# Storing rows as whole tiles and loading tokens by stretch in a fused attention, Fourier-mixing and feed-forward kernel

## The chip, the cores and the metric

The kernel runs on one core of one Trainium2 chip. The metric is device time in microseconds (us) of one execution; the time before is the median of three runs. A separate execution was taken with the hardware profiler, and all rows below come from that one.

## The reference

Inputs are q, k, v of 8 batches, 8 heads, 576 positions and 64 dimensions, and two weight matrices, 512x2048 and 2048x512. Per batch and head the attention is the sum of two parts: a pooled one (q, k, v averaged over groups of 4 positions, softmax over all 144 groups, the result repeated 4 times) and a local one (softmax over the 7 positions with |i-j| < 4). Heads are joined to rows x of 512 channels. Then

```
mixed = real(fft(fft(x, axis=1), axis=2))
u  = x + mixed
un = (u - mean(u)) / sqrt(var(u) + 1e-6)        # per row
out = u + max(un @ w_ch1, 0) @ w_ch2
```

## The kernel before

**Attention and mixing, batch by batch.** A batch has five *units* of the local attention (class `Unit`): each covers two windows of 64 positions that lie 57 apart, and gives rows of a tile `x` in SBUF. A window's first three and last three rows only serve as neighbours; the rows that count are 4 to 60 of a window, or 0 to 60 for the first of a half. The second half of a batch is computed in reversed order. Rows of the first half go to the tile `xa`, those of the second half to `xb`, 128 partitions (two windows) by 3 slots by 512 channels. The class `Pooled` computes the pooled part of a batch in four steps of two heads; its result `odt` is moved and stored by L337 to L341. The class `Mix` does the Fourier mixing of a batch: it adds `xa` and `xb` mirrored (`cross`, `fold`), multiplies by a sequence matrix (`sequence`) and a channel matrix (`mix`), and leaves the mixed rows in two tiles `oa` and `ob`.

**Three stores per batch.** What the feed-forward part needs goes to DRAM: `ud` (pooled rows, 1 transfer), `ul` (local rows, L640 to L650, 10 transfers) and `um` (mixed rows, L630 to L637, 5 transfers), in the order of tokens. One of the five for `um`, L635, takes partitions 1 to 127 of `ob`, 127 rows.

**Feed-forward.** The 4608 rows are cut into 36 tiles of 128 and 9 blocks of 4 tiles (class `Block`). A tile is loaded by SP from `ul` (L715), and GpSimd's (POOL's) queue adds `um` (L713) and `ud` (L711) to it by accumulating DMAs, in the order of the four tiles: four times `um`, then four times `ud`. DVE then takes the statistics (`stats`), normalises (`norm`), PE transposes (`turn`), and ACT and DVE split the result in two parts. Per block, 16 steps f follow: `first` (12 matmuls, L770), `high` on ACT, `low` on DVE, `second` (12 matmuls, L788 to L790). While block n is multiplied, block n+1 is loaded and prepared: the load of a tile waits until the output of block n-1 that lies in the same buffer has been stored (L798). The weights come as 64 quarters, four for each f (`raw`, fetched on SP at L150), and are decoded on ACT, POOL and DVE; 8 quarters are decoded during attention, 56 from its end on.

**What sets the order.** Every step is planned at a time in units of its own (the dictionary `AT`, 20 units per batch); all steps are sorted by that time and issued in that order. Each engine's queue, SP's and POOL's among them, runs its instructions in that order and stops at the first one that has to wait. All DMAs but the accumulating and the constant ones are issued by SP. The loads of the next batch's q and k (`qkT`, L367) and v (`vaug`, L371) therefore stand in the same queue as the stores of `um` (planned as `M.store`) and `ul` (`M.store_local`).

Of the kernel before, what the change touches and what calls it, by code (L numbers as in the profile page):

```python
# [8 lines left out]
F32 = mybir.dt.float32  # L9
# [4 lines left out]
ALU = mybir.AluOpType  # L14
# [5 lines left out]

PACE = 20
AT = {

    "pooled": (-1.19, 0.05, -1.8, -2.83, -3.64),
    "mix": (18.82, 18.19, 18.08),

    "local_steps": (0, 1.59, 2.96, 4.87, 6.03, 7.81, 9.34),
    "pooled_steps": (0, 1.56, 3.05, 4.81, 5.73, 7.85, 9.41),

    "qk": (-12.1, 2.19),  # L30
    "sums": (-2.01, 0.44),
    "sum_v": (-13.12, -6.44, -2.59, 2.41),
    "load_v": (0.51,),

    "store_pooled": (0.1, 0.2),
    "crosses": ((1, 4.9), (2, 8.0), (0, 9.2)),
    "folds": ((3, 4.3), (1, 5.9), (2, 8.5), (0, 10.0)),
    "splits": (0.37, 0.9, 1.3),
    "z": (10.2, 12.12, 12.81, 15.82),
    "sequence": (12.92, 1.78, 0.82, 1.82),  # L40
    "mixed": (20.36, 2.6, 0.6, 0.9, 1.5, 2.0, 2.6),
    "store_local": (9.6,),

    "ffn": (4.81, 1.67),

    "decode": (50.65, 9.96, 8.82, 1.2, 1.74),
    "decode_steps": (-1.38, 0.24, 0.83, 1.88, 2.96),
    "first_norms": (1.6, 0.81, 2.43, 1.1),
    "second_norms": (-0.15, 1.47, 0.8, 1.75),

    "add": (13.24, 1.0, 2.2),
}


# [5 lines left out]

TINY_HIGH = 1.125 * 2.0**-15
HUGE_HIGH = 2.0**16 * (1.875 - 2.0**-23)


@with_exitstack
def kernel(
# [34 lines left out]
    HS = S // 2  # L101
# [3 lines left out]

    dram = ctx.enter_context(tc.tile_pool(name="dram", bufs=1, space=DRAM))
    ud = [dram.tile([G, DM], F32, name=f"ud{b}") for b in range(B)]
    ul = [dram.tile([S, DM], F32, name=f"ul{b}") for b in range(B)]
    um = [dram.tile([S, DM], F32, name=f"um{b}") for b in range(B)]

    res = ctx.enter_context(tc.tile_pool(name="res", bufs=1))

# [96 lines left out]
    odt = pd.tile([GX, 2, DM + 2], F32, name="odt")  # L209
# [13 lines left out]
    xab = [[px.tile([P, NSL, DM + 2], F32, name=f"x{j}{i}") for j in "ab"] for i in range(2)]
    for ts in xab:
        for t in ts:
            nc.gpsimd.memset(t[:, :, DM:], 0.0)
        nc.gpsimd.memset(ts[1][W:, NSL - 1, :DM], 0.0)
# [16 lines left out]
    sums = {}  # L244

    class Pooled:
# [86 lines left out]

        def move(self):

            x = xab[self.b % 2][0]
            nc.sync.dma_start(out=odt[GH:GX, 0, :DM], in_=odt[W:GH, 1, :DM])  # L337
            nc.sync.dma_start(out=x[W:, NSL - 1, :DM], in_=odt[:W, 1, :DM])

        def store(self):  # L340
            nc.sync.dma_start(out=ud[self.b].rearrange("(t g) c -> g t c", t=2), in_=odt[:GH, :, :DM])  # L341

        def plan(self):
            b = self.b
# [13 lines left out]
    class Unit:  # L358
# [104 lines left out]

        def result(self):
            full = slice(0, P)
            xa, xb = (x[:, :, :DM] for x in xab[self.b % 2])
# [36 lines left out]
    outs = [P, P, NK1 - 2 * P]  # L503
# [9 lines left out]
    class Mix:  # L513
# [7 lines left out]

        def cross(self, t):
            pq = self.pq[t] = psq.tile([P, 2, HD], F32, name="pq", bufs=3)
            xa, xb = xab[self.b % 2]
# [26 lines left out]
            nc.gpsimd.tensor_sub(out=l, in0=self.x[t], in1=h.bitcast(F32))  # L551

        def split_z(self):
            xa, xb = xab[self.b % 2]
# [68 lines left out]


        def mirror(self, t):
            n = outs[t]
            for o, x in (self.o, self.o[::-1]):
                nc.scalar.copy(out=o[:n, t, HD + 1 :], in_=x[:n, t, HD - 1 : 0 : -1])

        def store(self):  # L630
            oa, ob = self.o
            u = um[self.b]
            nc.sync.dma_start(out=u[: 2 * P].rearrange("(t p) c -> p t c", t=2), in_=oa[:, :2])
            nc.sync.dma_start(out=u[2 * P : HS], in_=oa[: HS - 2 * P, 2])
            nc.sync.dma_start(out=u[HS : HS + P - 1], in_=ob[1:, 0])  # L635
            nc.sync.dma_start(out=u[HS + P - 1 : HS + 2 * P - 1], in_=ob[:, 1])
            nc.sync.dma_start(out=u[HS + 2 * P - 1 :], in_=ob[: HS - 2 * P + 1, 2])  # L637


        def store_local(self):  # L640
            for x, r0, first in zip(xab[self.b % 2], (0, HS - 1), (0, 1)):
                for n2 in range(2):
                    base = r0 + n2 * STEP
                    for lo, hi, n in ((4, 60, NSL - n2), (60, 61, NSL - n2 - (not n2 and not first))):
                        dst = ul[self.b][base + lo : base + hi, :]
                        dst = bass.AP(
                            tensor=dst.tensor, offset=dst.offset, ap=[dst.ap[0], [2 * STEP * DM, n], dst.ap[1]]
                        )
                        nc.sync.dma_start(out=dst, in_=x[n2 * W + lo : n2 * W + hi, :n, :DM])
                nc.sync.dma_start(out=ul[self.b][r0 + first : r0 + 4, :], in_=x[first:4, 0, :DM])  # L650
# [42 lines left out]
    class Block:  # L693
# [134 lines left out]
    folds = dict(AT["folds"])  # L828
# [149 lines left out]
STEP, WINDOW, NPAIR, SEQ, HEADS, DIM = 57, 64, 5, 576, 8, 64  # L978
# [71 lines left out]
```

## Time and profile before

| | |
|---|---|
| median of 3 runs | 1276.24 us (1273.78 to 1283.35) |
| profiled execution | 1278.39 us |
| its span in the trace | 1276.5 us |
| mean granted TensorE clock | 0.916 |
| instructions | 20617 |

The span runs from the first to the last instruction of the trace; the execution's time also holds the 1.9 us around it. The granted clock is a share of TensorE's upper level: 1.0 stands for 2.4 GHz, 0.5 for 1.2 GHz. DMA issues are rows of a queue (SPq, or POOL for GpSimd's) and tell how long the issue held that queue; how long the transfer took is seen in the chain of waits, or in what waited for it.

### The profile page before, as it was taken

The numbers are of one execution on the slowest core, as the hardware profiler recorded it, in microseconds if no ns is written. First come the engines' busy times: TensorE is split into PE (matmuls) and PEld (weight loads), VectorE is DVE, ScalarE is ACT, GpSimd is POOL, SyncE is SP. The second block draws the span as 40 slices with busy tenths as digits, with TensorE's granted clock in tenths as the row PEclk, the third lists the DMA queues.
The fourth block names the chain that finished last, engine by engine and source line by source line (L and its number), as shares of the span: only waits on it lengthen the run. The fifth ranks groups of instructions, "written<-read, shape, count | busy, mean of one in ns | idle before, by whom it ended". The sixth has DMA issues, their size and how long they took to land.

```text
span 1276.5 us, 20617 instructions
## 1 busy us (share of the span) xinstructions
PE 1134.8 (89%) x8304; PEld 950.6 (74%) x8304; DVE 529.4 (41%) x1218; ACT 366.7 (29%) x1102; POOL 276.8 (22%) x405
## 2 busy tenths in 40 slices
PE   5797778667587497999999999999999999999998
PEld 4676666657577375788888888888888888888887
DVE  3666547555464585983322122222222222221111
ACT  2656446364455243441101111111111111111010
POOL 2223223142331653663020020030020110200000
PEclk6778778796878698999999999999999999999999
DMA  9655474565734653445050050060140320500000
GB/s 289 177 161 157 148 223 121 156 178 165 197 94 116 171 139 106 129 130 123 10 131 3 1 132 1 1 132 1 65 68 1 91 42 1 127 6 1 34 1 33
DMA packets 57886, 123.02 MB, mean 96 GB/s; under 512 B 7296, under 2 KB 7424, under 8 KB 57536
## 3 DMA queue, kind: packets, MB, share of 16 engines
q1 hardware_dynamic: 44272, 92.17, 22.8%
q0 software_dynamic: 13520, 29.55, 13.1%
q8 instruction: 65, 1.06, 0.3%
q14 instruction: 29, 0.24, 0.1%
HBM read 89.89 MB, written 30.67 MB: 94 GB/s over the span
## 4 chain that ended last, share of the span: by engine, by line
PE 65%; DMA 16%; DVE 10%; ACT 4%; SPq 2%; issue 2%; POOL 1%; DVEq 0%; ACTq 0%; POOLq 0%
PE hps L770 28%; PE acc L788 10%; PE acc L790 9%; PE acc L789 9%; DMA qkT<-in_qk_dram 6%; DMA vsum<-in_vg_dram 2%; DMA ul<-xa 2%; DMA ul<-xb 2%; PE mix L609 2%; DMA raw<-in_wq_dram 2%; PE avd L313 1%; ACT sb L419 1%; DVE sums L385 1%; DMA um<-ob 1%; DVE wt L176 1%
## 5 line engine op out<-in xcount | busy, mean ns | idle before, releaser
L770 PE MATMUL hps<-unT,w1h 128*128 128x512 f32 x1152 | 312.2, 393 | 1.8 <-DVE unT L750 1.8
L778 DVE SCALAR_TENSOR_TENSOR hl<-hps,hh 128x512 fp32r<-128x512 f32 x144 | 99.2, 689 | 471.3 <-ACT hh L774 471.3
L770 PEld LDWEIGHTS hps<-unT,w1h 128*128 128x128 f32 x1152 | 216.5, 189 | 48.3 <-DVE unT L750 2.3
L788 PE MATMUL acc<-w2h,hh 128*128 128x512 f32 x576 | 228.2, 396 | 9.3 <-ACT hh L774 8.8
L774 ACT ACTIVATE hh<-hps 128x512 fp32r<-128x512 f32 x144 | 86.0, 597 | 510.9 <-PE hps L770 510.9
L790 PE MATMUL acc<-w2h,hl 128*128 128x512 f32 x576 | 225.7, 392 | 0.0
L789 PE MATMUL acc<-w2l,hh 128*128 128x512 f32 x576 | 225.6, 392 | 0.0
L770 PE MATMUL hps<-unT,w1l 128*128 128x512 f32 x576 | 155.7, 392 | 0.0
L788 PEld LDWEIGHTS acc<-w2h,hh 128*128 128x128 f32 x576 | 108.7, 189 | 33.2 <-ACT hh L774 9.2
L790 PEld LDWEIGHTS acc<-w2h,hl 128*128 128x128 f32 x576 | 108.5, 188 | 23.9 <-DVE hl L778 0.2
L770 PEld LDWEIGHTS hps<-unT,w1l 128*128 128x128 f32 x576 | 108.7, 189 | 23.6
L789 PEld LDWEIGHTS acc<-w2l,hh 128*128 128x128 f32 x576 | 108.8, 189 | 22.3
L726 POOL TENSOR_TENSOR rstd<-rstd,mhalf 128x1 f32<-128x1 f32 x36 | 20.3, 563 | 294.0 <-DVE rstd L725 294.0
L713 POOL DMA_DIRECT2D ut<-um x40 | 35.8, 1071 | 210.0 <-DMA ut<-ul 209.4
L385 DVE TENSOR_REDUCE sums<-qkT 128x224 f32<-128x896 f32 (+4 forms) x48 | 44.6, 949 | 70.1 <-DMA qkT<-in_qk_dram 69.6
L460 PE MATMUL av<-vaug,pT 64*64 64x65 f32 x1280 | 38.0, 262 | 38.4 <-DMA vaug<-in_vw_dram 36.4
L419 ACT ACTIVATE sb<-sc,mx 128x64 f32<-128x64 f32 x320 | 69.8, 329 | 1.3
L460 PEld LDWEIGHTS av<-vaug,pT 64*64 64x64 f32 x1280 | 31.0, 168 | 46.7 <-issue 41.2
L571 PE MATMUL y<-seqm,fh 128*128 128x290 f32 (+1 forms) x256 | 48.9, 341 | 16.0 <-DVE odt L328 7.3
L571 PEld LDWEIGHTS y<-seqm,fh 128*128 128x128 f32 (+1 forms) x256 | 42.7, 224 | 19.0 <-issue 8.4
L551 POOL TENSOR_TENSOR fl<-xeo,fh 128x512 fp32r<-128x512 f32 (+1 forms) x32 | 43.5, 1361 | 49.0 <-ACT fh L544 49.0
L268 PE MATMUL sp<-sums 64*72 64x144 f32 x256 | 29.8, 348 | 26.7 <-DVE sums L385 17.3
(97 smaller groups left out, 1414.5 us busy)
## 6 DMA issues: line engine op xcount, KB each, us to landing
qkT<-in_qk_dram SPq DMA_DIRECT2D x40, 512.0 KB
raw<-in_wq_dram SPq DMA_DIRECT2D x64, 256.0 KB
vaug<-in_vw_dram SPq DMA_DIRECT2D x40, 260.0 KB
out_dram<-ut SPq DMA_DIRECT2D x36, 256.0 KB
ut<-ul SPq DMA_DIRECT2D x32, 256.0 KB
ut<-um POOLq DMA_DIRECT2D x32, 256.0 KB, 5.7
ut<-ud POOLq DMA_DIRECT2D x32, 256.0 KB, 5.7
vsum<-in_vg_dram POOLq DMA_DIRECT2D x24, 292.5 KB, 7.3
```

Source lines behind the costliest of these rows:

```text
L385: nc.vector.tensor_reduce(out=to, in_=x[:, :, a - g0 : e - g0], axis=AX.X, op=ALU.add)
L419: nc.scalar.activation(out=self.sb[:, hp, h2], in_=sc[:, hp], func=AF.Exp, scale=0.125, bias=self.mx[:, h2, hp : hp + 1],)
L460: nc.tensor.matmul(av[n2 * W : (n2 + 1) * W, hp, :], pT[r, hp, n2], va[r, n2, hp, :], start=True, stop=True)
L551: nc.gpsimd.tensor_sub(out=l, in0=self.x[t], in1=h.bitcast(F32))
L571: nc.tensor.matmul(y, l, r, start=(i == 0), stop=(i == len(mms) - 1))
L713: nc.gpsimd.dma_start(out=u[r0 : r0 + m], in_=um[b][k0 : k0 + m, :], accum_op=ALU.add)
L770: nc.tensor.matmul(hps, a[:, c, :], unT[:, x, c, :], start=(i == 0), stop=(i == len(mms) - 1))
L774: nc.scalar.activation(out=hh, in_=self.hps[f], func=AF.Relu)
L778: nc.vector.scalar_tensor_tensor(out=hl, in0=self.hps[f], scalar=0.0, in1=self.hh[f].bitcast(F32), op0=ALU.max, op1=ALU.subtract)
L788: nc.tensor.matmul(acc, hh, w2h, start=start, stop=False)
L789: nc.tensor.matmul(acc, hh, w2l, start=False, stop=False)
L790: nc.tensor.matmul(acc, hl, w2h, start=False, stop=stop)
```

## The change

**Stores.** `xa` and `xb` become the two halves of one tile `x`, and `oa` and `ob` those of one tile `o`. `ul[b]` is now laid out as slot, half, partition, channel, and gets whole tiles, the rows that don't count included: one transfer of 128 partitions by 4 x 2 KB (1 MB) and one of 64 partitions by 2 x 2 KB (256 KB). `um[b]` is laid out as half, row: for each half one transfer of 128 partitions by 2 x 2 KB (512 KB) and one of 33 rows (66 KB). So 6 transfers instead of 15; `ud` is as before.

**Loads.** A tile's rows are picked out of `ul` by stretch, a stretch being the run of tokens that one window holds (61 or 57). `even_rows` shortens a piece until its number of rows has a divisor from 12 to 16 (or until it has 16 rows at most), and the rest is a piece of its own: 57 rows become 56 and 1. The loads from `um` are cut where a half ends.

**Order.** Most numbers of `AT` are changed. The pooled part of batch 0 moves 2.34 units later, so that on every engine its steps stand behind those of the local units that they stood ahead of; on SP, P0.move and P0.store stand behind one load of v and behind P2.sum_v0. In the other batches neighbouring steps change places. The fetches of quarters 9 and 10 stand ahead of the loads of block 1 on SP. The formulas for the loads and preparation of blocks 2 to 8 are unchanged; the step of the feed-forward plan goes from 1.67 to 1.64 units.

```diff
-    "pooled": (-1.19, 0.05, -1.8, -2.83, -3.64),
-    "mix": (18.82, 18.19, 18.08),
+    "pooled": (1.15, 0.05, -1.8, -2.74, -3.55),
+    "mix": (18.82, 18.55, 17.92),
...
-    "ffn": (4.81, 1.67),
-    "decode": (50.65, 9.96, 8.82, 1.2, 1.74),
+    "ffn": (3.75, 1.64),
+    "decode": (49.49, 9.96, 8.98, 1.2, 1.74),
...
-    "add": (13.24, 1.0, 2.2),
+    "add": (14.25, 2.77, 2.2),
...
+def even_rows(m):
+    while m > 16 and max(k for k in range(1, 17) if m % k == 0) < 12:
+        m -= 1
+    return m
...
-    ul = [dram.tile([S, DM], F32, name=f"ul{b}") for b in range(B)]
-    um = [dram.tile([S, DM], F32, name=f"um{b}") for b in range(B)]
+    ul = [dram.tile([NSL, 2, P, DM], F32, name=f"ul{b}") for b in range(B)]
+    um = [dram.tile([2, NSL * P, DM], F32, name=f"um{b}") for b in range(B)]
...
         def store(self):
-            oa, ob = self.o
-            u = um[self.b]
-            nc.sync.dma_start(out=u[: 2 * P].rearrange("(t p) c -> p t c", t=2), in_=oa[:, :2])
-            nc.sync.dma_start(out=u[2 * P : HS], in_=oa[: HS - 2 * P, 2])
-            nc.sync.dma_start(out=u[HS : HS + P - 1], in_=ob[1:, 0])
-            nc.sync.dma_start(out=u[HS + P - 1 : HS + 2 * P - 1], in_=ob[:, 1])
-            nc.sync.dma_start(out=u[HS + 2 * P - 1 :], in_=ob[: HS - 2 * P + 1, 2])
+            n = HS + 1 - 2 * P
+            for i in range(2):
+                u = um[self.b][i]
+                STORE.dma_start(out=u[: 2 * P].rearrange("(t p) c -> p t c", p=P), in_=self.o[:, i, : NSL - 1])
+                STORE.dma_start(out=u[2 * P : HS + 1], in_=self.o[:n, i, NSL - 1])
...
         def store_local(self):
-            for x, r0, first in zip(xab[self.b % 2], (0, HS - 1), (0, 1)):
...
+            x = xab[self.b % 2][:, :, :, :DM]
+            u = ul[self.b].rearrange("t j p c -> p (t j) c")
+            STORE.dma_start(out=u[:, :4], in_=x[:, :2].rearrange("p t j c -> p (t j) c"))
+            STORE.dma_start(out=u[:W, 4:], in_=x[:W, 2])
...
+                j, k = k0 // HS, k0 % HS
+                m = min(e - g, HS - k)
+                to = P - (e - g)
                 if part == 2:
+                    m = min(e - g, S - k0)
...
                 elif part:
-                    nc.gpsimd.dma_start(out=u[r0 : r0 + m], in_=um[b][k0 : k0 + m, :], accum_op=ALU.add)
+                    nc.gpsimd.dma_start(out=u[to : to + m], in_=um[b][j, k + j : k + j + m, :], accum_op=ALU.add)
                 else:
-                    nc.sync.dma_start(out=u[r0 : r0 + m], in_=ul[b][k0 : k0 + m, :])
+                    n = max(k + j - 4, 0) // STEP
+                    m = even_rows(min(m, STEP * n + STEP + 4 - k - j))
+                    r = k + j - STEP * n + (n % 2) * W
+                    nc.sync.dma_start(out=u[to : to + m], in_=ul[b][n // 2, j, r : r + m, :])
```

## Rows read from the trace of the kernel before

**Rows 1.** The page, its parts 1, 2 and 4: busy time and share of the span of each engine, the clock granted to TensorE in 40 slices of 31.9 us, and the shares of the chain that ended last.

```profile
PE 1134.8 (89%) x8304; PEld 950.6 (74%) x8304; DVE 529.4 (41%) x1218; ACT 366.7 (29%) x1102; POOL 276.8 (22%) x405
...
PEclk6778778796878698999999999999999999999999
...
PE 65%; DMA 16%; DVE 10%; ACT 4%; SPq 2%; issue 2%; POOL 1%; DVEq 0%; ACTq 0%; POOLq 0%
```

**Rows 2.** The chain of waits from 90 to 250 us, in order of time: start, length, what; the pieces of one batch that are no engine's work.

```profile
108.04 14.70 DMA um<-ob
122.75 5.95 DMA ul<-xb
...
129.67 9.19 DMA qkT<-in_qk_dram
```

**Rows 3.** The timeline of SP's own queue in the same batch: start, time the issue held SP, line, destination and source, count.

```profile
107.33 0.33 SPq L634 DMA_DIRECT2D um<-oa  x1
107.72 0.27 SPq L635 DMA_DIRECT2D um<-ob  x1
108.04 4.00 SPq L636 DMA_DIRECT2D um<-ob  x1
112.16 0.52 SPq L637 DMA_DIRECT2D um<-ob  x1
113.12 0.37 SPq L367 DMA_DIRECT2D qkT<-in_qk_dram  x1
113.56 2.73 SPq L649 DMA_DIRECT2D ul<-xa  x4
122.11 0.27 SPq L650 DMA_DIRECT2D ul<-xa  x1
```

**Rows 4.** Who waited for whom from 98.6 to 364.2 us, five batches: total us, times, longest.

```profile
DVE sums L385 <- DMA qkT<-in_qk_dram: 61.6, 18, 8.5
```

**Rows 5.** Busy time of the engines in three stretches, each bounded by two moves of the pooled rows (L337): one batch, five batches, and one of those five. Columns: stretch, its length, busy us (instructions) of PE, PEld, DVE, ACT, POOL, granted clock, DMA share, GB/s.

```profile
53.70:98.60 44.90, 39.24 (x562) 34.10 (x554) 29.08 (x81) 26.41 (x99) 12.35 (x18) 0.78 0.56 159
98.60:364.20 265.60, 194.45 (x2850) 171.69 (x2850) 151.65 (x425) 135.63 (x501) 74.07 (x107) 0.79 0.58 165
204.70:252.10 47.40, 32.92 (x525) 28.77 (x526) 28.70 (x81) 26.43 (x100) 13.59 (x20) 0.88 0.64 180
```

**Rows 6.** The timeline of SP at the end of attention, after the last local rows are computed.

```profile
422.45 2.95 SPq L649 DMA_DIRECT2D ul<-xa  x4
...
430.39 2.37 SPq L649 DMA_DIRECT2D ul<-xb  x4
...
433.76 2.72 SPq L715 DMA_DIRECT2D ut<-ul  x5
```

**Rows 7.** The chain of waits from 405 to 536 us, where decoding and the first FFN blocks run.

```profile
485.03 9.10 DMA raw<-in_wq_dram
...
508.80 2.71 DMA raw<-in_wq_dram
```

**Rows 8.** The timeline of PE: matmuls before which PE stood idle (in brackets: us idle and what ended it), and one group of the same matmuls, L460, without a wait before it.

```profile
14.67 1.24 PE L268 MATMUL sp<-sums 64*72 64x144 f32 x8 [9.38 <-DVE sums L385]
...
235.51 1.16 PE L460 MATMUL av<-vaug,pT 64*64 64x65 f32 x29 [4.70 <-DMA vaug<-in_vw_dram]
...
409.28 0.70 PE L460 MATMUL av<-vaug,pT 64*64 64x65 f32 x32
...
456.60 0.66 PE L741 MATMUL tpn<-ident,un 128*128 128x128 f32 x4 [2.05 <-DVE un L733]
...
495.49 0.80 PE L788 MATMUL acc<-w2h,hh 128*128 128x512 f32 x1 [8.80 <-ACT hh L774]
```

**Rows 9.** Busy time and granted clock (the number after POOL) in a stretch right behind the last of those waits.

```profile
497.00:499.00 2.00, 2.00 (x6) 1.58 (x5) 1.90 (x5) 1.17 (x3) 1.20 (x2) 0.50 0.07 16
```

**Rows 10.** The timelines of SP, POOL, DVE and PE while block 3 is loaded beside block 2's matmuls, and the same pair of rows (norm, turn) in two later blocks.

```profile
652.66 2.75 SPq L715 DMA_DIRECT2D ut<-ul  x5
656.36 1.77 POOL L713 DMA_DIRECT2D ut<-um  x2 [27.20 <-DMA ut<-ul]
661.83 3.55 POOL L711 DMA_DIRECT2D ut<-ud  x4 [0.36 <-issue]
667.64 0.69 DVE L722 BATCH_NORM_STATS2 st<-ut 128x6 f32<-128x512 f32 x1 [1.15 <-DMA ut<-ud]
669.48 0.55 DVE L733 TENSOR_SCALAR un<-ut,mv,rstd 128x512 f32<-128x512 f32 x1 [0.75 <-POOL rstd L726]
670.41 0.60 PE L741 MATMUL tpn<-ident,un 128*128 128x128 f32 x4
...
759.25 0.55 DVE L733 TENSOR_SCALAR un<-ut,mv,rstd 128x512 f32<-128x512 f32 x1 [0.73 <-POOL rstd L726]
759.87 0.64 PE L741 MATMUL tpn<-ident,un 128*128 128x128 f32 x4
...
936.59 0.55 DVE L733 TENSOR_SCALAR un<-ut,mv,rstd 128x512 f32<-128x512 f32 x1 [0.73 <-POOL rstd L726]
938.77 0.60 PE L741 MATMUL tpn<-ident,un 128*128 128x128 f32 x4
```

**Rows 11.** DMA issues on SP that touch the stored local rows: issue time in ns (shortest, median, longest), first and last start.

```profile
L715 SPq DMA_DIRECT2D ut<-ul x40: 319/408/1017, 287.7 to 1103.3; - x40
L649 SPq DMA_DIRECT2D ul<-xa x32: 398/600/1274, 58.4 to 424.8; - x32
```

More of the change, by code (lines that the diff above doesn't have):

```diff
@@ L22 @@
 AT = {
-    "pooled": (-1.19, 0.05, -1.8, -2.83, -3.64),
-    "mix": (18.82, 18.19, 18.08),
-    "local_steps": (0, 1.59, 2.96, 4.87, 6.03, 7.81, 9.34),
-    "pooled_steps": (0, 1.56, 3.05, 4.81, 5.73, 7.85, 9.41),
+    "pooled": (1.15, 0.05, -1.8, -2.74, -3.55),
+    "mix": (18.82, 18.55, 17.92),
+    "local_steps": (0, 1.66, 2.96, 4.76, 5.65, 7.95, 9.34),
+    "pooled_steps": (0, 1.56, 3.05, 4.81, 5.63, 7.85, 9.33),
     "qk": (-12.1, 2.19),
-    "sums": (-2.01, 0.44),
-    "sum_v": (-13.12, -6.44, -2.59, 2.41),
+    "sums": (-2.36, 0.44),
+    "sum_v": (-12.96, -6.64, -4.76, 2.36),
     "load_v": (0.51,),
     "store_pooled": (0.1, 0.2),
[L36 to L42, printed above, removed]
-    "ffn": (4.81, 1.67),
-    "decode": (50.65, 9.96, 8.82, 1.2, 1.74),
-    "decode_steps": (-1.38, 0.24, 0.83, 1.88, 2.96),
-    "first_norms": (1.6, 0.81, 2.43, 1.1),
-    "second_norms": (-0.15, 1.47, 0.8, 1.75),
-    "add": (13.24, 1.0, 2.2),
+    "crosses": ((1, 4.59), (2, 7.41), (0, 9.2)),
+    "folds": ((3, 5.97), (1, 4.28), (2, 8.26), (0, 10.0)),
+    "splits": (0.74, 0.9, 1.64),
+    "z": (9.51, 12.03, 12.81, 15.82),
+    "sequence": (12.92, 1.78, 0.82, 1.66),
+    "mixed": (20.32, 2.6, 0.2, 0.9, 1.47, 2.03, 2.91),
+    "store_local": (9.66,),
+    "ffn": (3.75, 1.64),
+    "decode": (49.49, 9.96, 8.98, 1.2, 1.74),
+    "decode_steps": (-1.47, 0.24, 0.83, 2.1, 2.96),
+    "first_norms": (0.57, 0.81, 2.43, 0.6),
+    "second_norms": (0.03, 1.47, 0.8, 1.83),
+    "add": (14.25, 2.77, 2.2),
 }
@@ L80 @@
     nc = tc.nc
+    STORE = nc.sync
     P = 128
@@ L220, in bank @@
         return banks[-1].tile([P, DM], F32, name=name, tag="ps")[:rows]
[L223 to L227, printed above, removed]
+    xab = [px.tile([P, NSL, 2, DM + 2], F32, name=f"x{i}") for i in range(2)]
+    for x in xab:
+        nc.gpsimd.memset(x[:, :, :, DM:], 0.0)
+        nc.gpsimd.memset(x[W:, NSL - 1, 1, :DM], 0.0)
     def pooled_at(b):
@@ L334, in move @@
         def move(self):
-            x = xab[self.b % 2][0]
-            nc.sync.dma_start(out=odt[GH:GX, 0, :DM], in_=odt[W:GH, 1, :DM])
-            nc.sync.dma_start(out=x[W:, NSL - 1, :DM], in_=odt[:W, 1, :DM])
+            x = xab[self.b % 2]
+            STORE.dma_start(out=odt[GH:GX, 0, :DM], in_=odt[W:GH, 1, :DM])
+            STORE.dma_start(out=x[W:, NSL - 1, 0, :DM], in_=odt[:W, 1, :DM])
         def store(self):
-            nc.sync.dma_start(out=ud[self.b].rearrange("(t g) c -> g t c", t=2), in_=odt[:GH, :, :DM])
+            STORE.dma_start(out=ud[self.b].rearrange("(t g) c -> g t c", t=2), in_=odt[:GH, :, :DM])
         def plan(self):
@@ L465, in result @@
             full = slice(0, P)
-            xa, xb = (x[:, :, :DM] for x in xab[self.b % 2])
+            xa, xb = (xab[self.b % 2][:, :, i, :DM] for i in range(2))
             if self.m < 2:
@@ L523, in cross @@
             pq = self.pq[t] = psq.tile([P, 2, HD], F32, name="pq", bufs=3)
-            xa, xb = xab[self.b % 2]
+            xa, xb = (xab[self.b % 2][:, :, i] for i in range(2))
             for i, (u, v) in enumerate(((xa, xb), (xb, xa))):
@@ L553, in split_z @@
         def split_z(self):
-            xa, xb = xab[self.b % 2]
+            xa, xb = (xab[self.b % 2][:, :, i] for i in range(2))
             z = self.z = psq.tile([P, NSL + 1, 2], F32R, name="z", bufs=1)
@@ L613, in copy_odd @@
             if self.o is None:
-                self.o = [pf.tile([P, NSL, DM], F32, name=f"o{part}", bufs=2) for part in "ab"]
-            nc.scalar.copy(out=self.o[1][: outs[t], t, : HD + 1], in_=self.ps[t, 1][:, : HD + 1])
+                self.o = pf.tile([P, 2, NSL, DM], F32, name="o", bufs=2)
+            nc.scalar.copy(out=self.o[: outs[t], 1, t, : HD + 1], in_=self.ps[t, 1][:, : HD + 1])
         def join(self, t):
@@ L619, in join @@
             even = self.ps[t, 0][:, : HD + 1]
-            oa, ob = (o[:n, t, : HD + 1] for o in self.o)
+            oa, ob = (self.o[:n, i, t, : HD + 1] for i in range(2))
             for o, op in ((oa, ALU.add), (ob, ALU.subtract)):
@@ L626, in mirror @@
             n = outs[t]
-            for o, x in (self.o, self.o[::-1]):
-                nc.scalar.copy(out=o[:n, t, HD + 1 :], in_=x[:n, t, HD - 1 : 0 : -1])
+            for i in range(2):
+                nc.scalar.copy(out=self.o[:n, i, t, HD + 1 :], in_=self.o[:n, 1 - i, t, HD - 1 : 0 : -1])
         def store(self):
-            oa, ob = self.o
-            u = um[self.b]
-            nc.sync.dma_start(out=u[: 2 * P].rearrange("(t p) c -> p t c", t=2), in_=oa[:, :2])
-            nc.sync.dma_start(out=u[2 * P : HS], in_=oa[: HS - 2 * P, 2])
-            nc.sync.dma_start(out=u[HS : HS + P - 1], in_=ob[1:, 0])
-            nc.sync.dma_start(out=u[HS + P - 1 : HS + 2 * P - 1], in_=ob[:, 1])
-            nc.sync.dma_start(out=u[HS + 2 * P - 1 :], in_=ob[: HS - 2 * P + 1, 2])
-        def store_local(self):
-            for x, r0, first in zip(xab[self.b % 2], (0, HS - 1), (0, 1)):
[L642 to L650, printed above, removed]
+            n = HS + 1 - 2 * P
+            for i in range(2):
+                u = um[self.b][i]
+                STORE.dma_start(out=u[: 2 * P].rearrange("(t p) c -> p t c", p=P), in_=self.o[:, i, : NSL - 1])
+                STORE.dma_start(out=u[2 * P : HS + 1], in_=self.o[:n, i, NSL - 1])
+        def store_local(self):
+            x = xab[self.b % 2][:, :, :, :DM]
+            u = ul[self.b].rearrange("t j p c -> p (t j) c")
+            STORE.dma_start(out=u[:, :4], in_=x[:, :2].rearrange("p t j c -> p (t j) c"))
+            STORE.dma_start(out=u[:W, 4:], in_=x[:W, 2])
         def plan(self):
@@ L706, in load @@
                 b, k0 = g // S, g % S
-                m = min(e - g, S - k0)
-                r0 = P - (e - g)
+                j, k = k0 // HS, k0 % HS
+                m = min(e - g, HS - k)
+                to = P - (e - g)
                 if part == 2:
+                    m = min(e - g, S - k0)
                     groups = ud[b][k0 // 4 : (k0 + m) // 4, :].unsqueeze(1).to_broadcast([m // 4, 4, DM])
-                    nc.gpsimd.dma_start(out=u[r0 : r0 + m], in_=groups, accum_op=ALU.add)
+                    nc.gpsimd.dma_start(out=u[to : to + m], in_=groups, accum_op=ALU.add)
                 elif part:
-                    nc.gpsimd.dma_start(out=u[r0 : r0 + m], in_=um[b][k0 : k0 + m, :], accum_op=ALU.add)
+                    nc.gpsimd.dma_start(out=u[to : to + m], in_=um[b][j, k + j : k + j + m, :], accum_op=ALU.add)
                 else:
-                    nc.sync.dma_start(out=u[r0 : r0 + m], in_=ul[b][k0 : k0 + m, :])
+                    n = max(k + j - 4, 0) // STEP
+                    m = even_rows(min(m, STEP * n + STEP + 4 - k - j))
+                    r = k + j - STEP * n + (n % 2) * W
+                    nc.sync.dma_start(out=u[to : to + m], in_=ul[b][n // 2, j, r : r + m, :])
                 g += m
```

## The prediction, made before the changed kernel was run

> **What bounds the kernel now.** I read the page first. PE is busy 89% of the span, but the granted clock stays at 0.9 or more only from slice 17 on, 510 us [rows 1]: behind lies feed-forward, where PE has hardly a gap, before it attention, mixing and decoding, where it has. A change in storing can win only there, and lose anywhere. The chain of waits gives 16% of the span (204 us) to DMAs [rows 1], so I followed it through one batch: from 108 to 139 us no engine is its bottleneck. A transfer to um (L636's) takes 14.70 us, then one to ul 5.95, then a load of qkT 9.19 [rows 2].
>
> SP's queue says why. L635 (254 KB, 127 partitions) is issued in 0.27 us; the next issue holds SP 4.00 us instead of some 0.33, and the eighth DMA behind L635 (one each of L636, L637 and qkT, four of L649, then L650) starts only at 122.11, when that transfer has landed [rows 2, 3]. At the end of attention, with no qkT load between, the eighth is the first store of xb, and it too waits until 430.39 [rows 6]. So SP has eight DMAs in flight, and the ninth waits for the first. What stands behind is the next batch's qkT, and DVE, in whose queue the sums of qkT stand, waits 61.6 us for it in five batches [rows 4]. L635's 254 KB thus took 14.4 us (107.72 to 122.11), 18 GB/s, and L636, issued behind it, landed no sooner; a whole 256 KB tile of weights takes 2.71 us [rows 7].
>
> The Trainium skill, "DMA: Bandwidth & Descriptors", section "Why a DMA increments its semaphore by 16 and not by 1", gives the reason: a DMA runs on the largest k up to 16 engines that divides its outer size, and 127 rows give k = 1. The trace agrees as far as 18 GB/s goes; by its rate of about 27 GiB/s per engine (an estimate) 9 us would do, and the gain below would be a third smaller.
>
> **Part 1, stores.** 15 transfers become 6, none of 127 rows; the odd ones have 33 rows, like L637, which takes 0.52 us to issue [rows 3]. Bytes hardly change (um 1156 KB as before, ul 1280 for 1136). The L635 wait goes in each batch.
> *Five batches* (98.6 to 364.2). Upper bound: DVE's whole 61.6 us. But something comes next. The batch before them, with ul stores and no um stores, ran in 44.9 us, PE busy 39.2 of it [rows 5]; five such are 225 us against 265.6. That is -41. Lower bound: the one batch of the five that took 47.4 us in spite of the wait shows that waits overlap other work, and its own excess over 44.9 is 2.5; I put the weak end at -20, half.
> *End of attention.* From 417.92 to 433.2 SP is in the last stores; then the loads of block 1 begin [rows 6]. Six transfers at 0.6 us end some 12 us earlier; 1.25 MB then need up to 8 us to land at the mean 165 GB/s [rows 5], so the loads begin 4 to 12 us earlier, 9 say. Block 1 now needs 21 pieces instead of 5 loads (part 2), +7 us, felt by the fetches behind them, but not by those of quarters 9 and 10, now ahead: I count 4. Together -5, between -10 and 0.
> *Last um stores*, among the weight fetches: the raw issued behind L637 takes 9.10 us, and PE stands idle 8.80 us [rows 7, 8]; behind it PE runs at half clock (0.50) for 4 us [rows 9], 2 us more. Taken: -9, between -11 and -4, as four stores still stand there.
>
> **Part 2, loads.** Cutting tokens 0 to 4607 by the new code gives 180 loads on SP instead of 40, 18 to 22 per block for blocks 2 to 8 (mean 20), and 48 um loads on POOL instead of 40. The place where this counts is the start of each block. In block 3's loading, SP begins at 652.66; um starts at 656.36; POOL's queue runs four um issues and then ud, whose first starts at 661.83, 9.2 us after SP; the statistics wait for it on DVE until 667.64, norm ends at 670.03, and PE turns at 670.41 [rows 10]. The slack is 0.4 us; in block 4 it is 0.07, in block 6 1.6 [rows 10]. PE's queue is in order, so nearly every us by which the first ud comes later is a us of PE, seven times (blocks 2 to 8), plus whatever `low` of the running block, behind the statistics on DVE, adds.
> New offset of that ud: 19 spacings on SP + landing of the last piece + um issues of the last tile + a gap of 0.36. Spacing c: issues of ut<-ul have a median of 408 ns, stores in pieces 600 ns [rows 11], and back to back a row every 0.39 us is possible (107.33 to 107.72) [rows 3]; I take 0.45, nearest to the same line's row, between 0.39 and 0.67. Landing: 2.7 us [rows 7], for 3.7 with four whole tiles at once. um issues: 0.88 each (1.77 for 2 [rows 10]), 1.4 on average, 1.3 us. So 8.6 + 2.7 + 1.3 + 0.36 = 12.9. Then 5.8 to the statistics and 2.4 to the end of norm: 21.1 us after SP begins, where PE turns at 17.75. A stall of 3.3 us per block, 23 in seven. Bounds: with c 0.39 and a landing of 2.2 us, 12; with c 0.67, 52.
> *Clock.* A gap of 2.05 us cost PE no clock, one of 4.70 did (29 matmuls of L460 then took 1.16 us, where 32 took 0.70 without a wait) [rows 8]. 3.3 lies between: +7, between 0 and 14 (2 us per block).
> *Block 0* is loaded during attention, 19 pieces for 4: 15 more at 0.45 us in front of qkT loads, in four places where SP mostly waits for engines anyway: +1, between 0 and 5.
>
> **Part 3, order.** Batch 0's pooled steps, all of them and its three DMAs, go behind local units. PE's first idle, 9.38 us waiting for sums [rows 8], can now hold local scores; against that, P0.move stands behind P2.sum_v0 on SP, which waits for the buffer that P0's last values free, so just before P0.move's own data: 1 us at most. The other exchanges are between neighbours. No row prices them; bounded by that idle and by one DMA landing: -2, between -8 and +5.
>
> **Sum** against the profiled execution of 1278.4: -41 - 5 - 9 + 23 + 7 + 1 - 2 = -26, so 1252. It lies 2.2 above the median of the runs, so I predict 1250.
>
> **Rivals.**
> *A, the pieces hide.* Issue at 0.39 and quick landing leave about 1.7 us per block, no clock loss, and attention comes nearer to the 61.6: -52 - 5 - 9 + 12 - 2 + 1 = -55, 1223 (median basis 1221). For: SP is idle before each block, small loads land fast. Against: zero slack in most blocks.
> *B, the wait moves on.* With qkT in time, batches take 49 us instead of 45 because PE and DVE are in order and the um stores still wait for ACT: -21 - 5 - 9 + 31 - 2 = -6, 1272 (1270). For: DVE and ACT are half busy in every batch and hand over to each other [rows 5]. It also covers the case that the 33-row transfers or whole tiles bring no quicker SP.
> *C, slower: the pieces on SP at the head of each block.* If a piece costs 0.67 us, as the stores in pieces did, the stall is 7.5 us plus 2 of clock, 66 in seven, block 1 gets 5 more and block 0 5: -41 - 2 + 0 - 9 + 66 + 5 = +19, 1297 (1295). It decides from about 0.56 us a piece, where the seven stalls eat the 54 us won. For: the local rows' stores, pieces of 56 rows and of one, held SP 600 ns [rows 11]. The Trainium skill, "DMA: Bandwidth & Descriptors", section "Rules for kernel authors", says the same: coalesce many small transfers, as those under 64 KB are mostly overhead. At the 2 us of fixed cost that its section "Anatomy of one DMA" gives for GpSimd's DMAs, one after another, 20 pieces would be 40 us per block and the kernel far slower; but eight are in flight at once [rows 3], which makes it 5 us, below the issue time, and leaves the sum.
>
> **How the numbers follow.** Forecast 0.45, A 0.25, B 0.15, C 0.15. Predicted 1250. The forecast's own range is 1228 to 1270 from the terms' bounds, not all at one end. The range for 8 in 10 takes in most of A and B and leaves out the far half of C: 1217 to 1284. A measurement here can tell about 1% from no change, 12.8 us, so faster means under 1263.5 and slower over 1289: faster 0.25 (A) + 0.35 (forecast) + 0.03 (B) = 0.63; same 0.10 + 0.11 + 0.03 (C) = 0.24; slower 0.12 (C) + 0.01 = 0.13.
>
> **What would show it.** Right, if no issue of SP holds 4 us in the um stores, DVE's wait for qkT falls from 61.6 to under 15 us, and the moves of the pooled rows come about 45 us apart. The stall shows as PE idle before `turn` of the first tile of blocks 2 to 8, released by DVE's norm, near 3 us each, and as first ud issues near 13 us after SP's first piece; A if there is none, C if they are 7 us or more with the clock at 0.50 behind. The forecast fails if batches stay above 50 us, or if the blocks, now 89.5 us apart (759.87 and 938.77 are two of them [rows 10]), come more than 97 apart.

## The result and the profile after

The changed kernel takes 1199.64 us (median of 4 runs, 1195.84 to 1203.31); the kernel before, beside it, takes 1275.12. The ratio is 0.9395 [0.9344, 0.9447]: 75 us faster, where 26 were forecast, and below the range of 1217 to 1284. The profiled execution of after took 1203.31 us, its span is 1201.5. A trace is of one execution, which can lie off its kernel's median (1234.27 for 1226.42 with the old order below, 1289.33 for 1277.60 with the old um), so a few us between two traces say little.

The page of after, the lines of [rows 1]:

```profile
PE 1108.2 (92%) x8304; PEld 927.0 (77%) x8304; DVE 526.5 (44%) x1218; ACT 366.0 (30%) x1102; POOL 277.8 (23%) x411
...
PEclk9788899997978999999999999999999999999999
...
PE 55%; DMA 8%; SPq 4%; DVE 3%; issue 1%; POOL 1%; ACT 0%; POOLq 0%; DVEq 0%; ACTq 0%
```

The same 8304 matmuls keep PE busy for 26.6 us less, and the share of DMAs in the chain of waits is halved. I cut both spans at the same events: the moves of the pooled rows (L337, one per batch) and the first `turn` of blocks 2 and 8.

| stretch | before | after | difference | in the forecast's sum |
|---|---|---|---|---|
| to the first move | 53.7 | 52.3 | -1.4 | (order: -2 in all) |
| one batch | 45.0 | 40.4 | -4.6 | none |
| five batches | 265.6 | 198.6 | -67.0 | -41 |
| last batch | 46.8 | 34.4 | -12.3 | none |
| last move to block 2's first turn, less that turn's stall | 197.1 | 177.9 | -19.2 | -14 |
| stall there, block 2's first turn to block 8's, to the end | 668.4 | 697.9 | +29.5 | +30 (and +1 for block 0, loaded during attention) |

The batches, by the view of [rows 5]: stretch, length, busy us (instructions) of PE, PEld, DVE, ACT, POOL, granted clock, DMA share, GB/s.

```profile
52.30:92.70 40.40, 37.15 (x558) 32.23 (x554) 27.09 (x76) 26.58 (x98) 12.65 (x19) 0.81 0.61 175
92.70:291.30 198.60, 169.99 (x2864) 149.93 (x2858) 150.68 (x425) 134.07 (x499) 70.67 (x108) 0.91 0.75 224
291.30:325.70 34.40, 30.91 (x566) 27.95 (x557) 23.35 (x76) 25.31 (x94) 14.07 (x20) 1.00 0.59 157
```

Against [rows 5], PE's busy time in five batches fell from 194.5 to 170.0 at nearly the same number of matmuls (2850 and 2864 in the trace), as the granted clock rose from 0.79 to 0.91; its idle time fell from 71.1 to 28.6. So 24.5 of the 67.0 us are shorter matmuls, about what the clock gives (194.5 times 0.79 by 0.91 is 169), and 42.5 are gaps that closed.

SP's own queue in the second of these batches, and at the end of attention (start, time the issue held SP, line, what):

```profile
99.58 0.32 SPq L635 DMA_DIRECT2D um<-o  x1
99.94 0.38 SPq L634 DMA_DIRECT2D um<-o  x1
100.43 0.72 SPq L635 DMA_DIRECT2D um<-o  x1
101.19 0.53 SPq L367 DMA_DIRECT2D qkT<-in_qk_dram  x1
101.77 0.80 SPq L641 DMA_DIRECT2D ul<-x  x1
102.61 0.65 SPq L642 DMA_DIRECT2D ul<-x  x1
103.36 1.74 SPq L371 DMA_DIRECT2D vaug<-in_vw_dram  x1
...
334.00 3.83 SPq L151 DMA_DIRECT2D raw<-in_wq_dram  x3
337.93 9.13 SPq L712 DMA_DIRECT2D ut<-ul  x21
```

In [rows 3] the stretch from L635 to the last ul store took from 107.72 to beyond 122; here the stores and the qkT load are through in 3.7 us (99.58 to 103.26). At the end block 1's loads begin 12.2 us behind the last move (337.93 less 325.73), before 22.8 [rows 6]: 10.6 sooner, where I had 9.

The waits of after, for [rows 4] (the five batches, then the trace from 505 to 1042 us; total us, times, longest):

```profile
DVE sums L385 <- DMA qkT<-in_qk_dram: 15.2, 9, 4.9
...
PE tpn L738 <- DVE un L730: 20.8, 7, 4.5
```

The second line is the price of the pieces: a wait that PE did not have in blocks 2 to 8 before.

### The profile page after: what moved, and what is told of

It is laid out like the page before. It is cut to its first block, busy times and chain, and to the rows that moved or that the text cites. A ratio compares the mean times of both kernels' runs of the same rounds, so it can differ in the third digit from the quotient of the medians.

```text
span 1201.5 us, 20868 instructions
## 1 busy us (share of the span) xinstructions
PE 1108.2 (92%) x8304; PEld 927.0 (77%) x8304; DVE 526.5 (44%) x1218; ACT 366.0 (30%) x1102; POOL 277.8 (23%) x411
## 4 chain that ended last, share of the span: by engine, by line
PE 55%; DMA 8%; SPq 4%; DVE 3%; issue 1%; POOL 1%; ACT 0%; POOLq 0%; DVEq 0%; ACTq 0%
PE hps L767 26%; PE acc L785 9%; PE acc L786 9%; PE acc L787 9%; DMA ut<-ud 4%; DMA ut<-ul 3%; SPq L712 3%; DVE ut L791 1%; PE tpn L738 1%; PE mix L609 1%; POOL ut L707 1%; DVE st L719 1%; DVE hl L775 0%; DVE un L730 0%; ACT hh L771 0%
## 5 line engine op out<-in xcount | busy, mean ns | idle before, releaser
L785 PEld LDWEIGHTS acc<-w2h,hh 128*128 128x128 f32 x576 | 109.7, 190 | 22.8
L707 POOL DMA_DIRECT2D ut<-um x48 | 41.9, 1006 | 237.0 <-DMA ut<-ul 200.3
L738 PE MATMUL tpn<-ident,un 128*128 128x128 f32 x144 | 25.6, 309 | 35.1 <-DVE un L730 35.1
L744 ACT CAST unT<-tpn 128x512 fp32r<-128x512 f32 x36 | 21.1, 586 | 118.1 <-PE tpn L738 118.1
L738 PEld LDWEIGHTS tpn<-ident,un 128*128 128x128 f32 x144 | 19.5, 158 | 42.5 <-DVE un L730 38.5
L551 POOL TENSOR_TENSOR fl<-xeo,fh 128x512 fp32r<-128x512 f32 (+1 forms) x32 | 41.6, 1303 | 28.6 <-ACT fh L544 28.6
L571 PE MATMUL y<-seqm,fh 128*128 128x290 f32 (+1 forms) x256 | 44.3, 318 | 4.0 <-DVE x L479 3.1
L313 PE MATMUL avd<-vsum,ptd 72*72 72x65 f32 x512 | 42.2, 239 | 6.3 <-DMA vsum<-in_vg_dram 6.3
```

Of the source, the lines that this page charges most:

```text
L313: nc.tensor.matmul(av[:, t, hl, :], self.pts[h0][hl][:, kt, t * GH : (t + 1) * GH], self.vs[:, kt, h0 + hl, :], start=(kt == 0), stop=(kt ...
L571: nc.tensor.matmul(y, l, r, start=(i == 0), stop=(i == len(mms) - 1))
L707: nc.gpsimd.dma_start(out=u[to : to + m], in_=um[b][j, k + j : k + j + m, :], accum_op=ALU.add)
L738: nc.tensor.transpose(tp[:, c * P : (c + 1) * P], self.un[i][:, c * P : (c + 1) * P], ident)
L785: nc.tensor.matmul(acc, hh, w2h, start=start, stop=False)
```

## The experiments

Each ratio is to the kernel before, run beside it (medians of 1276.84 to 1277.22; 1275.12 beside after). "Five batches" is the stretch between the moves of [rows 5].

| kernel | us | ratio | five batches | DVE waits for qkT in them | last batch |
|---|---|---|---|---|---|
| before | 1276 | 1 | 265.6 | 61.6 | 46.8 |
| before, 127 rows split | 1208.54 | 0.948 | 220.6 | 19.8 | 38.4 |
| before, new um | 1207.98 | 0.9452 | 221.5 | 17.9 | 40.0 |
| before, new order | 1262.04 | 0.9885 | 261.7 | 72.8 | 45.6 |
| after, old order | 1226.42 | 0.9604 | 202.9 | 6.2 | 39.8 |
| after | 1199.64 | 0.9395 | 198.6 | 15.2 | 34.4 |
| after, old um | 1277.60 | 1.0019 | 248.0 | 61.6 | 44.0 |
| before, L635 on ACT's queue | 1287.30 | 1.007 | 267.2 | 69.4 | 49.2 |
| before, ul loads in pieces | 1323.31 | 1.0385 | 267.9 | 66.1 | 46.4 |
| after, preparation later | 1172.97 | 0.9197 | 197.8 | 15.8 | 34.4 |
| after, ud sooner | 1209.65 | 0.9492 | 196.0 | 13.1 | 34.4 |
| after, no `even_rows` | 1290.99 | 1.0103 | 197.7 | 17.3 | 35.0 |
| before, new um and order, later | 1192.01 | 0.933 | 210.1 | 24.0 | 35.8 |

### Which store held attention up

**Only the 127-row transfer cut**, into 112 and 15 rows; all else as before.

```diff
-            nc.sync.dma_start(out=u[HS : HS + P - 1], in_=ob[1:, 0])
+            nc.sync.dma_start(out=u[HS : HS + 112], in_=ob[1:113, 0])
+            nc.sync.dma_start(out=u[HS + 112 : HS + P - 1], in_=ob[113:, 0])
```

> The kernel before, old order, with only the 127-row store cut into 112 and 15 rows (16 transfers per batch instead of 15; the loads stay whole). Theory S (that one transfer is the cause): the attention part gains what the change gained and the feed-forward part pays nothing for pieces: 1178 to 1200 us. Rival N (it is the number of transfers on SP, 15 against 6, that cost): 1255 to 1278 us.

One DMA more, and 68 us less: 0.948 [0.9416, 0.9543], 9 us above the range expected and far from the rival's. The view of the DMA engines tells why. Its first line, shown here, gives the busy share of the 16 engines in 40 slices, in tenths (here 0.4 us each). Before, 107 to 123 us (the stretch of [rows 3]):

```profile
DMA  1015100100000188559897999995897742100001
```

The same view of 16 us around the stores (106 to 122) with the transfer split:

```profile
DMA  2005397895899957989758999975888779799994
```

And of after (99 to 115):

```profile
DMA  9987799997794979999999999999999999999999
```

Before, the engines stand nearly still twice, while SP is held in L636's issue (108 to 112) and again from about 120 on, until L635 has landed at 122.11. One engine of 16 is 0.06 of them, and the share there is 0 to 1 tenth. The Trainium skill, "DMA: Bandwidth & Descriptors", section "Why a DMA increments its semaphore by 16 and not by 1", would put 127 rows on one engine and 112 on sixteen; the rows agree.

**The new um alone** in the kernel before (tile of halves, four stores, loads cut at the half).

> The kernel before, old order, with the new layout, stores and loads of um alone (4 transfers instead of 5, none of 127 rows); ul stays in the order of tokens with its 10 transfers. Theory S: as the split, 1175 to 1200 us, because ul's ten stores cost SP time but no wait. Rival N: 1245 to 1270 us.

0.9452 [0.9407, 0.9497], as with the split alone, and again 8 us above the expected range. So um's part of the change is worth what the 127-row transfer cost; the fewer transfers add nothing here.

**The order alone**, and **the changed kernel with the old order**: only the dictionary `AT` exchanged.

> The kernel before with the new numbers of AT alone; stores and loads as before. Theory S (the stores did it: the 127-row transfer on one DMA engine is gone, order is minor): 1265 to 1285 us, DVE's wait for qkT still near 60 us in five batches, batches still about 53 us. Rival O (the new order is what made batches of 39.7 us, where the stores alone would have given 45): 1240 to 1255 us.

> The changed kernel with the old numbers of AT: new stores, new loads. Theory S: 1193 to 1212 us, five batches still within 10 us of the 198.6 us that the changed kernel takes for them. Rival O: 1220 to 1235 us, batches near 45 us.

Alone the order gives 14.8 us, 0.9885 [0.9844, 0.9927], between the two ranges expected; on the new storage 26.8 (1226.42 to 1199.64), some 12 either way. By its time the changed kernel with the old order falls in rival O's range, by its batches (202.9, or 40.6 each, not 45) in theory S's: the order is not minor, but the short batches come from the stores. By the spans of the two kernels (31.0 us apart) the order is 3.7 to the first move, 2.6 in the next batch, 4.3 in the five, 5.4 in the last, 8.1 between block 2's and block 8's first turns (543.2 to 535.1), and 6.9 in what is left.

With these the five batches add up: the new um -44.1 (265.6 to 221.5), the new ul behind it, old order still, -18.6 (to 202.9), the order -4.3 (to 198.6). The -18.6 goes with a shorter queue on SP: with the split, the ten ul stores still hold SP from 109.59 to 117.99, 8.4 us, where the two of after take 1.5 (above), and DVE's wait for qkT falls from 17.9 to 6.2. That this is its cause is argued; no run changed the ul stores alone.

### Two ways from the slow transfer to qkT

In [rows 2, 3] the slow transfer could delay qkT in two ways: it holds one of eight places, and the ninth DMA waits (my prediction's account), or the transfers behind it wait on the one engine for their own share. Two kernels tell these apart. **The old um in the changed kernel**, with two ul stores behind the 127 rows:

> The changed kernel with the old layout, stores and loads of um, the 127-row transfer among them; ul and order as changed. Only two ul stores stand behind it, so the eighth DMA behind it comes much later in SP's queue. If the wait for one of eight places in flight is what cost, most of the gain stays: 1205 to 1225 us. If the transfer also holds up every other transfer that uses its DMA engine, qkT lands late all the same: 1245 to 1275 us.

**L635 issued from ACT's queue** in the kernel before:

```diff
-            nc.sync.dma_start(out=u[HS : HS + P - 1], in_=ob[1:, 0])
+            nc.scalar.dma_start(out=u[HS : HS + P - 1], in_=ob[1:, 0])
```

> The kernel before, with the 127-row store alone issued from ACT's queue instead of SP's; it still runs on one DMA engine. If SP's held queue and its eight places were the cost: 1205 to 1225 us, as with the split. If the backlog of that one engine is, which every other transfer also has to use: 1255 to 1280 us, and DVE's wait for qkT in five batches above 45 us.

Neither keeps the gain: 1.0019 [0.9983, 1.0054], where after has 0.9395, and 1.007 [1.004, 1.010], 3 and 7 us above the slower of the two ranges expected. But they lose it in different ways. With the old um in the changed kernel SP hardly waits for a place. SP's waits for um in five batches (total us, times, longest):

```profile
SPq L151 <- DMA um<-o: 2.5, 3, 1.2
SPq L367 <- DMA um<-o: 1.8, 4, 1.2
SPq L715 <- DMA um<-o: 1.0, 1, 1.0
SPq L371 <- DMA um<-o: 0.6, 2, 0.4
```

That is 5.9 us, against 30.3 in the kernel before by the same view. Yet L636, issued just behind L635 on the same queue, lands after 14.70 us: by the trace's semaphore records fifteen of its sixteen shares have landed by 105.91, the last at 116.56, just behind L635 (115.93). In the kernel before it is the same (fifteen by 114.93, the last at 122.74). A load of qkT issued later, at 118.82, takes 12.12, where it took 9.19 in [rows 2]. Its chain of waits:

```profile
101.86 14.70 DMA um<-o
...
118.82 12.12 DMA qkT<-in_qk_dram
```

SP's own queue:

```profile
102.92 4.03 SPq L637 DMA_DIRECT2D um<-o  x1
```

So here the transfers queue up under the slow one, and SP is held by its issues behind it too (L637's 4.03 us, like L636's 4.00 in [rows 3]); how much each of these two costs was not separated. From ACT's queue it is the reverse. The chain of waits of that kernel:

```profile
103.72 18.52 DMA um<-ob
...
128.44 7.57 DMA qkT<-in_qk_dram
```

SP's own queue:

```profile
103.65 0.41 SPq L636 DMA_DIRECT2D um<-ob  x1
104.19 1.28 SPq L637 DMA_DIRECT2D um<-ob  x1
105.51 0.35 SPq L367 DMA_DIRECT2D qkT<-in_qk_dram  x1
106.31 2.86 SPq L649 DMA_DIRECT2D ul<-xa  x4
109.33 0.47 SPq L650 DMA_DIRECT2D ul<-xa  x1
122.26 2.22 SPq L649 DMA_DIRECT2D ul<-xb  x4
```

And what SP waited for in five batches:

```profile
SPq L649 <- DMA um<-ob: 67.7, 5, 14.8
```

L635 is issued on ACT at 103.72, the start of the 18.52 us in the chain. No issue of SP is held long any more. Counted with L635, L650 is the ninth DMA from L636 on, and it starts at 109.33: L636 had landed within 5.7 us (fifteen shares by 106.71, the last at 109.31). The next, L649 at 122.26, is the ninth from L635, and starts when that has landed (122.24). So the eight places, eight semaphores of the program in the trace, are shared by both queues, and moving the transfer did not free its place, as the expectation had taken for granted. SP then stands still for 67.7 us, and DVE waits 69.4 for qkT.

Each way alone thus loses in five batches about what the split wins there (45.0): 49.4 against after, and 267.2 us for 265.6. In the kernel before both are at work. Of the kernels run, those in which the transfer is short remove both; a store from GpSimd's queue was not tried.

### The pieces on SP

The start of block 3 in after, against [rows 10]: SP, POOL, DVE and PE (in brackets the idle time before, and what ended it).

```profile
550.77 7.35 SPq L712 DMA_DIRECT2D ut<-ul  x22
...
562.92 1.64 POOL L707 DMA_DIRECT2D ut<-um  x2 [1.73 <-DMA ut<-ul]
563.96 4.14 POOL L705 DMA_DIRECT2D ut<-ud  x4
...
569.38 0.69 DVE L719 BATCH_NORM_STATS2 st<-ut 128x6 f32<-128x512 f32 x1 [5.10 <-DMA ut<-ud]
571.22 0.55 DVE L730 TENSOR_SCALAR un<-ut,mv,rstd 128x512 f32<-128x512 f32 x1 [0.75 <-POOL rstd L723]
...
571.83 0.66 PE L738 MATMUL tpn<-ident,un 128*128 128x128 f32 x4 [3.46 <-DVE un L730]
665.83 1.11 PE L738 MATMUL tpn<-ident,un 128*128 128x128 f32 x4 [2.76 <-DVE un L730]
...
946.91 0.66 PE L738 MATMUL tpn<-ident,un 128*128 128x128 f32 x4 [2.37 <-DVE un L730]
1041.04 1.11 PE L738 MATMUL tpn<-ident,un 128*128 128x128 f32 x4 [4.50 <-DVE un L730]
```

The first ud is issued 13.2 us after SP begins (12.9 forecast, 9.2 before), and PE stands idle before each of the seven first turns, 2.29 to 4.50 us, 20.8 in all. At five of them the granted clock falls to 0.50 for some 3.4 us; at the two shortest (2.29 and 2.37) it stays at 1.00. From block 2's first turn to block 8's, PE's busy time shows what that costs. Before, in the columns of [rows 5]:

```profile
608.13:1117.72 509.59, 509.59 (x2282) 419.35 (x2281) 127.73 (x235) 66.79 (x115) 60.23 (x78) 1.00 0.23 50
```

After:

```profile
505.92:1041.04 535.12, 516.61 (x2281) 423.60 (x2281) 127.82 (x235) 66.80 (x115) 64.42 (x83) 0.99 0.23 48
```

25.5 us longer: 18.5 idle, 7.0 of clock (four gaps in this stretch have the lower level behind them, 1.75 us each).

**Pieces in the kernel before**: ul's loads cut at 28 rows, some 20 per block, nothing else.

```diff
+                    m = min(m, 28)
                     nc.sync.dma_start(out=u[r0 : r0 + m], in_=ul[b][k0 : k0 + m, :])
```

> The kernel before with each load from ul cut into pieces of at most 28 rows, some 20 per block; stores, um and order as before. The pieces alone cost what they cost in the changed kernel: 3 to 5 us per block, 1296 to 1312 us. Rival A (pieces hide): 1274 to 1284 us.

1.0385 [1.0334, 1.0437], 46 us, 11 above the range expected: seven stalls of 27.8 us in all, 31.9 between the two turns, 10.8 up to the first of them. The Trainium skill, "DMA: Bandwidth & Descriptors", section "Rules for kernel authors", has it so: coalesce many small transfers. The run agrees.

**Preparation later**: statistics, norm and turn of the next block planned later, so that PE's queue has other matmuls ahead of the turn.

```diff
-                v = starts[n] + 12 + i * (t - starts[n] - 18) / TILES
+                v = starts[n] + 15.3 + i * (t - starts[n] - 21) / TILES
```

> The changed kernel with the preparation of blocks 2 to 8 planned 3.3 units (one step f, about 5.4 us) later; loads as they are. If PE's stalls before the first turn of each block (20.8 us in seven in the changed kernel, up to 2 us of half clock behind each) come from ud arriving late, they vanish: 1168 to 1180 us. If something else sets them (bank, clock), 1192 to 1204 us.

1172.97, 0.9197 [0.9154, 0.924]: 26.7 us below the changed kernel, and the best of all. PE's timeline shows block 3's first turn without a wait:

```profile
570.63 0.60 PE L738 MATMUL tpn<-ident,un 128*128 128x128 f32 x4
```

**ud sooner**: each tile's ud issued soon behind its um, instead of behind all four um.

```diff
-                for part in range(3):
-                    at(starts[n] + 6 + 0.5 * i + 2 * part, blocks[n + 1].load, i, part)
+                for part, u in enumerate((0, 2, 2.7)):
+                    at(starts[n] + 6 + 0.5 * i + u, blocks[n + 1].load, i, part)
```

> The changed kernel with POOL's order changed in blocks 2 to 8: the ud of a tile follows one tile behind its um, not behind the um of all four tiles. If ud waits in POOL's queue for the last pieces of the fourth tile, the statistics of the first tile come 4 us or more sooner and the stalls vanish: 1168 to 1182 us. If the first tile's own um is what is late, 1190 to 1204 us.

This idea fell: 1209.65, 0.9492 [0.9454, 0.953], about 10 us above after and above both ranges expected, with stalls of 24.3 in all. POOL's timeline in block 3's loading:

```profile
567.25 0.92 POOL L705 DMA_DIRECT2D ut<-ud  x1 [1.87 <-DMA ut<-um]
570.13 0.88 POOL L705 DMA_DIRECT2D ut<-ud  x1 [1.96 <-DMA ut<-um]
570.69 0.90 POOL L723 TENSOR_TENSOR rstd<-rstd,mhalf 128x1 f32<-128x1 f32 x1
```

And DVE's:

```profile
564.20 0.69 DVE L719 BATCH_NORM_STATS2 st<-ut 128x6 f32<-128x512 f32 x1
...
571.63 0.55 DVE L730 TENSOR_SCALAR un<-ut,mv,rstd 128x512 f32<-128x512 f32 x1 [6.33 <-POOL rstd L723]
```

The statistics come 5.2 us sooner (564.20 for 569.38), but the norm needs `rstd`, which POOL raises to its power, and POOL's queue holds that behind the ud issues of tiles 3 and 4, which wait for um. The wait moved from one queue to another.

**Without `even_rows`**: 12 or 13 pieces per block instead of some 20, of up to 61 rows.

```diff
-                    m = even_rows(min(m, STEP * n + STEP + 4 - k - j))
+                    m = min(m, STEP * n + STEP + 4 - k - j)
```

> The changed kernel without even_rows: 112 loads from ul instead of 180, 12 or 13 per block, but stretches of 57 rows (3 engines, if the number of engines is the largest divisor up to 16) and of 61, 47 or 43 (1 engine). If transfers on few engines are slow, as the 127-row store was, the stalls at the first turns grow past 6 us each: 1225 to 1270 us. If the number of pieces is what costs: 1180 to 1195 us.

Fewer pieces, and 91 us slower than after: 1290.99, 1.0103 [1.0076, 1.0131], 21 above the range expected for slow pieces. Its waits, in the whole trace:

```profile
PE tpn L738 <- DVE un L730: 104.1, 12, 18.8
```

SP's timeline, the 13 pieces of block 3:

```profile
573.85 7.74 SPq L712 DMA_DIRECT2D ut<-ul  x13
```

And the DMA engines' view from 573 to 589 us:

```profile
DMA  9999974431164211121298799999630000000000
GB/s 389 404 353 389 374 241 133 102 138 61 77 138 189 87 77 77 72 77 72 77 154 148 174 210 251 266 236 231 133 56 21 15 15 15 20 15 21 26 26 26
```

The last 4 us move 15 to 26 GB/s, under a tenth of the engines, and not much more than the 18 GB/s of the 127-row transfer: the long tail of transfers on few of them. The 13 pieces hold SP no shorter than the 22 of after (7.74 us for 7.35); here a piece's row count decides.

**New um, new order and later preparation**, with ul as before:

> The changed kernel's um part and order, with the preparation of blocks 2 to 8 planned 3.3 units later, but ul as before: ten stores per batch, whole loads. If the ten ul stores cost some 18 us in five batches (as between the kernels of e4 and e2) and the pieces nothing once the preparation is later: 1183 to 1197 us, above e5's 1173. If whole-tile stores of ul are worth nothing: 1163 to 1176 us.

1192.01, 0.933 [0.9314, 0.9345], 19 us above the best version, 12.3 of them in the five batches. So ul as whole tiles pays once its pieces are hidden; 19 is less than the 26.7 that the stalls cost, so in the change as it stands the ul part loses some 8 us by these runs (1199.64 against 1192.01).

## Why the prediction was wrong

**Place and cause were right.** The 127-row transfer was what attention stood behind, and the eight places are one way from it to qkT, as I had them; I saw that L636 landed no sooner, but did not count the other, the queue on the engine under it, which keeps the loss where places are free (1.0019). Of my signs, no issue of SP holds 4 us any more, the batches are shorter than 45 us (39.7), and DVE's wait for qkT missed its 15 narrowly (15.2).

**The step that failed** is the floor of the five batches: "The batch before them, with ul stores and no um stores, ran in 44.9 us, PE busy 39.2 of it; five such are 225 us against 265.6." As the price of the 127-row transfer its number was near: the split gives 220.6, -45.0 for -41. The view of [rows 5] for the split:

```profile
97.85:318.50 220.65, 178.75 (x2879) 157.30 (x2879) 151.59 (x427) 135.41 (x501) 74.18 (x107) 0.88 0.70 199
```

Its make-up was not: five such batches have PE busy 196.2 us and idle 28.3, the split 178.8 and 41.9. The granted clock, 0.88 for that batch's 0.78, made up for the gaps that stayed, so the near number is in part luck. And that batch had the ten ul stores in it, and the change takes eight of them away; I counted 15 transfers becoming 6 and priced only one of the fifteen. They held SP for 8.4 us per batch where two take 1.5; the new ul and the order are worth 22.9 more (18.6 and 4.3), above the new um's 44.1. A batch that still has the removed work in it is no floor.

**The upper bound failed with it.** "DVE's whole 61.6 us" was no bound, for the gain was 67.0: when gaps close, the granted clock rises, and 24.5 us came out of PE's busy time. I read clock in feed-forward, where it costs, and not in attention, where it could give back. That this is the clock's own share is read from the busy times; no run held the clock fixed.

**The last batch was left out.** [rows 4] end where it begins, and I gave it nothing; it fell by 12.3, by 8.4 with the split alone. It too has a 127-row store in it, and what stands behind is a load of v. Before, from 364.2 to 411 us:

```profile
PE av L460 <- DMA vaug<-in_vw_dram: 5.3, 1, 5.3
```

With the split this wait is gone. Together with the first two stretches (-6.0; by the runs the order's, 3.7 and 2.6) that is 18 us that the sum did not have.

**The end of attention** was a size: -14 for a measured -19.2 without the stall, of which the split alone gives 16.7 (180.4 us). The loads began 10.6 us sooner, where I had 9.

**The pieces were right in sum and path**: +30, measured +29.5 (the 1 for block 0 can't be told apart). Stall 3.3 each for 3.0, clock 7 for 7.0 between the turns, the first ud at 12.9 for 13.2, and moving the preparation gives 26.7 back. Within the 12.9 two errors cancel, which is luck: the 22 pieces of block 3 took 0.33 us each and not 0.45, less than the lower bound of 0.39, so the last was issued 7.0 us after the first where I had 8.6; but from there POOL waited 5.2 us for the last data (until 562.92), where I had 2.7. Rival A, in which the pieces hide, and rival C, in which they eat the gain, are both refuted by the seven stalls; rival B by batches of 39.7 us (198.6 by five), where it asked for 49. **The order** was put at -2, between -8 and +5, from one idle of 9.38 us; it is 15 us alone and 27 here (some 12 either way), and the bounds, one idle and one landing, did not see that steps change places in every stage. The bytes of part 1 are slightly off (um and ul had 1152 KB each before, not 1156 and 1136); nothing hangs on them.

So of the 49 us by which the sum (-26) misses the spans' difference (-75.0), the five batches are 26, the other batches 18, the end of attention 5, and the pieces 1 or 2 the same way, less the 2 that stood for the order.

## What to carry to other kernels

Look first at the number of rows of every transfer: one with an awkward count can cost more than many small ones, and cutting it in two, by one more line, gave 68 us by itself; the whole change gave 75, with some 30 lost to the pieces. When a change removes several things, a stretch of the old trace serves as a floor only if it holds none of them. And if a load comes some microseconds later (4.0 here), plan what needs it as much later too, before paying for the stall.

## What was not expected of the hardware

A 254 KB transfer on one DMA engine delays a whole tile behind it on the same queue to 14.70 us, where one of weights takes 2.71 [rows 7]; with L635 on another queue it no longer does (under 5.7), but the eight places are common to both. Of the seven PE gaps of after, those of 2.29 and 2.37 us kept the granted clock at 1.00 (2.4 GHz), the one of 2.61 and the four longer ones brought 0.50 (1.2 GHz) for about 3.4 us, sometimes from the first matmul behind the gap on (665.83, a turn of 1.11 us), sometimes a microsecond later (571.83, 0.66).
